# Attention banks, GpSimd's share and a direct first expert chunk in a three-stage kernel on one Trainium2 core

## Chip, core and metric

The kernel runs on one core of a Trainium2 chip. The metric is device time in microseconds (us) of one execution. Below, PE is TensorE, ACT is ScalarE, DVE is VectorE, POOL is GpSimd and SP is SyncE, which issues all DMAs.

## What is computed

Three layers follow each other on 2 x 768 = 1536 tokens of width 512:

```python
# 1. attention in chunks of 32 queries, with 16 keys to the left, 8 to the right and 8 memory keys
scores = scale * q_c @ k_full.T
a = exp(scores - max(scores)); a = a / (sum(a) + 1e-09)
out[:, :, chunk] = a @ v_full
# 2. a feed-forward layer, d_ff = 2048, with a rational activation
h = x @ w_in
P = a[0] + a[1]*h + a[2]*h**2 + a[3]*h**3
Q = 1 + abs(b[0])*abs(h) + abs(b[1])*h**2
x = (P / (Q + 1e-6)) @ w_out
# 3. four experts, d_ff = 1024, all applied to all tokens, weighted by normalised domain_probs
out = sum(p[:, e:e+1] * (relu(x @ w1[e]) @ w2[e]) for e in range(4))
```

Everything is float32 in and out; `w_in` and `w_out` arrive as 64-bit floats and are turned into 32-bit ones by three integer operations on DVE (L349, L355, L361).

## The kernel before

**Precision.** Each operand of a large product is split into a high half, rounded by a copy on ACT (L278), and a low half, the difference, on POOL or DVE (L323). A product of two tiles is three matmuls: high x high, low x high, high x low (`PAIRS`). All large matmuls are 128x128 by 128x512.

**Attention.** The work is cut into 24 units of 64 rows by 2 heads and 4 chunks (`Unit`), eight per block of 512 tokens. A unit loads its keys, queries and values into one tile `w`, then goes through scores on PE (L421, L424), the maximum on DVE (`peaks`, L430), its scaling (`peaks2`, L436), four exponentials on ACT (L440), addition of 1e-9 and reciprocal (`norm1`, L446, and `norm2`, L449), the normalisation on POOL (`norm3`, L453), the transposition on PE (L459), the copy of the probabilities on ACT or DVE (`probs`, L278, L279) and the product with the values on PE (L476). ACT and DVE then write the high and low halves of x (L545, L550). Each unit takes three PSUM banks. `psum_buf` gives units of block 0 (0 to 7) six banks in turn, two of tag `att` and four of tag `acc`; later units have the two `att` banks.

**Stage A** (layer 2) has 48 steps `StepA`: a block and a tile f of 128 hidden columns. The first product (`first_ops`, L566) has 12 matmuls into a bank `h` or `att`; the activation runs through ACT, DVE and POOL (L630 to L664), among it `ln`, the linear term B1*|h| + B0 (L656, ACT) and the product `de` on POOL (L660); its halves g feed the second product (`second_ops`, L672) of 12 matmuls into four `acc` banks, `LAG` = 3 steps later. Four tiles f go round the three blocks, then the next four in the opposite order, so that the blocks end in the order `LAST` = PA, PB, LONE (blocks 2, 1, 0): PA is complete eight steps, PB four steps before the end.

**Stage B** (layer 3) has 16 chunks `Chunk` of two tiles f of one expert. For PA and PB together the first product of a chunk is a 2 x 2 block product done with seven products (`product`, L786, 6 matmuls each) of sums of x (`plan_sums_x`, L717) and sums of weights (`plan_sums_w`, L717), put together on DVE (`plus`, L842). LONE has two direct products (L566, 12 matmuls each). ACT and DVE form the halves of relu (`gated`, L881, L884). Then each block has a second product of 24 matmuls over four `acc` banks (`second`, L905), which DVE adds to the output (L920 in chunk 0, L922 later).

**What sets the order.** All operations are given to a planner (`Plan`) with the engines on which each may run and a cost for each. PE's operations have keys, which `tick` hands out in a list written by hand. The planner then lists the operations: of those that can start, the earliest, and among equals the most urgent. Every engine runs its list in that order, and DMAs are issued by SP in that order too. Rings of buffers (`BUFS`) are taken in the order of need. At the start, before and between attention work, zero products of 128x512 (`turn_over`, L291) keep PE occupied where the plan has a gap, up to the unit `FU`:

```python
for a, b in zip(pe, pe[1:]):
    if a.n == last:
        break
    n = int((b.start - a.end - FGAP) / 0.216)
    if n > 0:
        fill[a] = min(n, 16)
```

Here `last` is the one zero product that is planned behind the values of unit `FU`.

## Time and profile before

| what | us |
|---|---|
| median of three runs | 863.58 (862.87 to 864.3) |
| the profiled execution | 864.07 |
| its span, first to last instruction | 862.2 |
| outside the span | 1.87 |
| PE busy | 837.8 (97%) |
| DVE busy | 637.8 (74%) |
| ACT busy | 380.3 (44%) |
| POOL busy | 339.9 (39%) |

The profile is of one execution. Matmuls overlap, so that a busy PE is not PE at its peak: twelve matmuls in a row are read best from the distance between the starts of such rows. A "releaser" is the instruction whose end the waiting one needed last. Times are counted from the start of the span. Attention lies in the first 104 us, stage A goes to about 325 us with its last second products behind that, stage B to the end.

### The profile page before, as it was taken

The numbers are of one execution on the slowest core, as the hardware profiler recorded it, in microseconds if no ns is written. First come the engines' busy times: TensorE is split into PE (matmuls) and PEld (weight loads), VectorE is DVE, ScalarE is ACT, GpSimd is POOL, SyncE is SP. The second block draws the span as 40 slices with busy tenths as digits, with TensorE's granted clock in tenths as the row PEclk, the third lists the DMA queues.
The fourth block names the chain that finished last, engine by engine and source line by source line (L and its number), as shares of the span: only waits on it lengthen the run. The fifth ranks groups of instructions, "written<-read, shape, count | busy, mean of one in ns | idle before, by whom it ended". The sixth has DMA issues, their size and how long they took to land.

```text
span 862.2 us, 11387 instructions
## 1 busy us (share of the span) xinstructions
PE 837.8 (97%) x4205; PEld 666.9 (77%) x4208; DVE 637.8 (74%) x982; ACT 380.3 (44%) x819; POOL 339.9 (39%) x273
## 2 busy tenths in 40 slices
PE   7899999999999997899999999999999999999998
PEld 5676788888888885688888888888888888888886
DVE  6988798999988779974766766765765765765754
ACT  6988887867778766420320320320330330330310
POOL 3454476656667759800330330330330330330300
PEclk9889999999999999999999999999999999999999
DMA  9966021212122001110101101101101101100003
GB/s 345 370 208 233 2 98 50 73 50 74 49 74 65 10 0 51 49 49 1 49 1 49 49 1 49 50 2 48 49 5 46 49 12 38 49 20 6 2 1 146
DMA packets 21912, 55.42 MB, mean 64 GB/s; under 512 B 3936, under 2 KB 3936, under 8 KB 21856
## 3 DMA queue, kind: packets, MB, share of 16 engines
q1 hardware_dynamic: 21856, 54.69, 18.6%
q8 instruction: 33, 0.54, 0.3%
q14 instruction: 23, 0.19, 0.1%
HBM read 51.54 MB, written 3.15 MB: 63 GB/s over the span
## 4 chain that ended last, share of the span: by engine, by line
PE 85%; DVE 5%; ACT 4%; DMA 2%; POOL 2%; issue 1%; SPq 0%; ACTq 0%; POOLq 0%; DVEq 0%
PE acc L905 30%; PE att L566 16%; PE acc L672 13%; PE h L786 9%; PE h L566 8%; PE att L786 7%; ACT w L440 1%; ACT w L278 1%; DMA w<-q 1%; DMA w<-qk 1%; DVE w L323 1%; POOL tu L717 1%; POOL w L323 0%; DVE ts L647 0%; DMA stg<-w 0%
## 5 line engine op out<-in xcount | busy, mean ns | idle before, releaser
L323 POOL TENSOR_TENSOR w<-stg,w 128x512 fp32r<-128x512 f32 x64 | 96.5, 1518 | 331.5 <-ACT w L278 331.5
L922 DVE SCALAR_TENSOR_TENSOR p<-acc,pr,p 128x512 f32<-128x512 f32 x180 | 135.1, 751 | 107.1 <-PE acc L905 106.8
L905 PE MATMUL acc<-w,g 128*128 128x512 f32 x768 | 181.8, 397 | 1.6 <-DVE p L920 1.6
L905 PEld LDWEIGHTS acc<-w,g 128*128 128x128 f32 x768 | 144.8, 189 | 36.1 <-issue 2.0
L566 PE MATMUL att<-x,w 128*128 128x512 f32 x612 | 149.3, 395 | 0.5 <-DVE ts L842 0.5
L672 PE MATMUL acc<-g,w 128*128 128x512 f32 x576 | 145.4, 398 | 1.9 <-POOL g L323 1.8
L566 PEld LDWEIGHTS att<-x,w 128*128 128x128 f32 x612 | 114.6, 187 | 29.1 <-issue 0.9
L672 PEld LDWEIGHTS acc<-g,w 128*128 128x128 f32 x576 | 107.3, 188 | 28.5 <-POOL g L323 2.7
L278 ACT ACTIVATE ts<-h 128x512 f32<-128x512 f32 x16 | 9.6, 598 | 246.1 <-PE h L786 246.1
L905 PE MATMUL acc<-w,gb 128*128 128x512 f32 x384 | 92.0, 397 | 0.0
L566 PE MATMUL h<-x,w 128*128 128x512 f32 x348 | 90.8, 406 | 0.0
L905 PEld LDWEIGHTS acc<-w,gb 128*128 128x128 f32 x384 | 72.5, 189 | 17.0
L323 POOL TENSOR_TENSOR g<-ts,g 128x512 fp32r<-128x512 f32 x48 | 68.5, 1428 | 38.5 <-ACT g L278 38.1
L660 POOL TENSOR_TENSOR ts<-ts,tu 128x512 f32<-128x512 f32 x48 | 63.6, 1325 | 43.6 <-ACT ts L656 40.1
L566 PEld LDWEIGHTS h<-x,w 128*128 128x128 f32 x348 | 65.2, 192 | 15.3
L786 PE MATMUL h<-x,w 128*128 128x512 f32 x192 | 50.3, 396 | 2.3 <-ACT g L278 1.6
L786 PE MATMUL att<-x,w 128*128 128x512 f32 x192 | 50.1, 395 | 1.0 <-DVE ts L647 1.0
L786 PE MATMUL h<-w 128*128 128x512 f32 x192 | 49.2, 391 | 0.7 <-DVE w L323 0.7
L323 POOL TENSOR_TENSOR w<-y,w 128x512 fp32r<-128x512 f32 x34 | 47.3, 1395 | 4.4 <-ACT w L278 3.6
L786 PEld LDWEIGHTS h<-x,w 128*128 128x128 f32 x192 | 35.8, 187 | 11.7 <-ACT g L278 2.0
L278 ACT ACTIVATE w<-tu 128x512 fp32r<-128x512 f32 x32 | 20.1, 632 | 53.8 <-POOL tu L717 49.6
L786 PEld LDWEIGHTS att<-x,w 128*128 128x128 f32 x192 | 35.9, 188 | 9.8 <-DVE ts L647 1.4
(114 smaller groups left out, 1188.2 us busy)
## 6 DMA issues: line engine op xcount, KB each, us to landing
stg<-w SPq DMA_DIRECT2D x64, 512.0 KB, 3.6
w<-kv SPq DMA_DIRECT2D x32, 256.0 KB, 5.6
w<-q SPq DMA_DIRECT2D x16, 256.0 KB, 5.3
w<-qk SPq DMA_DIRECT2D x8, 400.0 KB, 6.2
out<-p SPq DMA_DIRECT2D x12, 256.0 KB, 2.0
w<-v SPq DMA_DIRECT2D x8, 256.0 KB, 7.3
pr<-prob SPq DMA_DIRECT2D x1, 24.0 KB, 3.8
cf<-coef SPq DMA_DIRECT2D x1, 3.0 KB, 7.0
```

Of the source, the lines that this page charges most:

```text
L278: return lambda o, i: ACT.activation(o, i, AF.Copy)
L323: engines[op.eng].tensor_tensor(out=dst[:, 1], in0=src, in1=dst[:, 0].bitcast(F32), op=ALU.subtract)
L440: ACT.activation(k(n), P1.ap[:, n * KB : (n + 1) * KB], AF.Exp, scale=SCALE, bias=nm()[:, n : n + 1], accum_out=sm()[:, n : n + 1],)
L566: PE.matmul(s.h.ap, wt[w].ap[:, 0, a, k * 128 : (k + 1) * 128], xs[k].ap[:, b], start=(k == 0 and n == 0), stop=(k == KT - 1 and n == 2),)
L660: lambda: POOL.tensor_tensor(out=s.ap, in0=s.ap, in1=u.ap, op=ALU.mult), [ln], [s, u],
L672: PE.matmul(ps, wt[f].ap[:, 1, a, d * 128 : (d + 1) * 128], g.ap[:, b], start=start, stop=stop)
L717: lambda: engines[o.eng].tensor_tensor(out=out(), in0=in0(), in1=in1(), op=op),
L786: PE.matmul(ps.ap, left(a, k), right(b, k), start=k == 0 and n == 0, stop=k == 1 and n == 2,)
L905: PE.matmul(ps.ap, gs[j][0].ap[:, a, d * 128 : d * 128 + 128], wt[f].ap[:, 1, b], start=j == 0 and n == 0, stop=j == 1 and n == 2,)
L922: DVE.scalar_tensor_tensor(out=y, in0=ps.ap, scalar=p, in1=y, op0=ALU.mult, op1=ALU.add)
```

## The change

It consists of these parts:

- **Banks.** `psum_buf` gives the six banks in turn to units 0 to 11 (`RU` = 12), not 0 to 7.
- **Small operations.** `peaks2` and `norm1`, 128x4 each and 24 of each, go from DVE to POOL.
- **Linear term.** `ln` may run on ACT or POOL; the planner chooses. It puts 31 of 48 on POOL.
- **Zero products** are placed up to unit 11, in place of 5: 20 in all, in place of 16.
- **Direct first chunk.** Chunk 0 of stage B forms the first products of PA and PB directly (`direct`), four of 12 matmuls for seven of 6, and needs no sums. They stand between the last three second products of stage A. The splits of x now cover all 12 tiles (10 before) and are planned ahead of the sums of x.
- **Costs.** A matmul counts 0.2325 in the plan (`MM`), and the costs of many operations are other numbers; two lines of that are shown.

```diff
+MM = 0.2325
-FU = 5
+FU = 11
+RU = 12
...
             self.hp, self.half = divmod(r, 2)
 
         def psum_buf(self):
-            if self.blk:
+            if self.u >= RU:
                 return bank("att")
             Unit.turn = (getattr(Unit, "turn", -1) + 1) % 6
             return bank((["att"] * 2 + ["acc"] * 4)[Unit.turn])
...
                 )
             def peaks2():
-                DVE.tensor_scalar(out=nm(), in0=nm(), scalar1=SCALE, scalar2=None, op0=ALU.mult)
+                POOL.tensor_scalar(out=nm(), in0=nm(), scalar1=SCALE, scalar2=None, op0=ALU.mult)
             def exps():
                 for n in range(NQ):
...
                     )
             def norm1():
-                DVE.tensor_scalar(out=sm(), in0=sm(), scalar1=1e-9, scalar2=None, op0=ALU.add)
+                POOL.tensor_scalar(out=sm(), in0=sm(), scalar1=1e-9, scalar2=None, op0=ALU.add)
             def norm2():
                 DVE.reciprocal(out=sm(), in_=sm())
...
-            o1 = add([("PE", 0.68)], scores, [*ready, o_mask, o_ident], [T], [P1], key=t_scores)
+            o1 = add([("PE", 0.75)], scores, [*ready, o_mask, o_ident], [T], [P1], key=t_scores)
             o = add([("DVE", 0.33)], peaks, [o1], [P1], [st])
-            o = add([("DVE", 0.07)], peaks2, [o], [st])
+            o = add([("POOL", 0.15)], peaks2, [o], [st])
...
     def first_ops(s, w, xs, ready, t):
-        s.h = bank("h" if s.i < 2 * GS[0] + 3 or s.i % 4 < 2 else "att")
+        s.h = bank(s.tag if hasattr(s, "tag") else "h" if s.i < 2 * GS[0] + 3 or s.i % 4 < 2 else "att")
         def go(k):
             for n, (a, b) in enumerate(PAIRS):
...
                     after, uses,
                 )
+            def linear():
+                if ln.eng == "ACT":
+                    ACT.activation(s.ap, u.ap, AF.Identity, scale=B1, bias=B0)
+                else:
+                    POOL.tensor_scalar(out=s.ap, in0=u.ap, scalar1=B1, scalar2=B0, op0=ALU.mult, op1=ALU.add)
+
             ln = add(
-                [("ACT", 0.7)],
-                lambda: ACT.activation(s.ap, u.ap, AF.Identity, scale=B1, bias=B0), [ab], [u], [s],
+                [("ACT", 0.7), ("POOL", 0.75)],
+                linear, [ab], [u], [s],
             )
             de = add(
                 [("POOL", 1.23)],
...
                 )
 
             self.g = {}
+            if not c:
+                self.direct(("h", "att", "h", "att"), (PA, PB))
+                self.direct(("h", "att"), (LONE,))
+                return self.seconds()
             m1, p1 = product(1, "h")
             self.gate = p1
             u2 = Buf("ts", [128, BLK], F32)
...
             m4, p4 = product(4, "h")
             c21, o21 = plus(u3, m4, [o22, p4])
             self.gated(1, PA, c21, [o21], "g")
-            for j, f in enumerate(self.fs):
-                r = SimpleNamespace(i=1002)
-                o = first_ops(
-                    r, f, [x2[LONE, k] for k in range(KT)], [x_ready[LONE, k, 3] for k in range(KT)],
-                    t["F", j],
-                )
-                self.gated(j, LONE, r.h, [o], "gb")
-            for b in sorted(LAST, key=lambda b: t["S", b]):
+            self.direct(("att", "att"), (LONE,))
+            self.seconds()
+
+        def direct(self, tags, blocks):
+            tags = list(tags)
+            for b in blocks:
+                for j, f in enumerate(self.fs):
+                    r = SimpleNamespace(tag=tags.pop(0))
+                    o = first_ops(
+                        r, f, [x2[b, k] for k in range(KT)], [x_ready[b, k, 3] for k in range(KT)],
+                        self.t["F", b, j],
+                    )
+                    if b != LONE:
+                        self.gate = getattr(self, "gate", o)
+                    self.gated(j, b, r.h, [o], "gb" if b == LONE else "g")
+
+        def seconds(self):
+            for b in sorted(LAST, key=lambda b: self.t["S", b]):
                 self.second(b)
 
         def gated(self, j, blk, h, after, tag):
...
             chunks[c].order(tick, x)
     def a_second():
-        t2[ending.pop(0)] = tick(2.592)
+        t2[ending.pop(0)] = tick(12 * MM)
     seven = [("P", i) for i in (1, 2, 6, 7, 5, 3, 4)]
-    products(0, *seven[:2])
-    a_second()
-    products(0, *seven[2:5])
-    a_second()
-    products(0, *seven[5:])
-    a_second()
-    products(0, ("S", PA), ("S", PB), ("F", 0), ("F", 1))
+    lone = ("F", LONE, 0), ("F", LONE, 1)
+    for b in (PA, PB):
+        for j in range(2):
+            products(0, ("F", b, j))
+            if ending:
+                a_second()
+    products(0, ("S", PA), ("S", PB), *lone)
     products(1, *seven)
     products(0, ("S", LONE))
-    products(1, ("F", 0), ("F", 1), ("S", PA), ("S", PB), ("S", LONE))
+    products(1, *lone, ("S", PA), ("S", PB), ("S", LONE))
     for c in range(2, NC):
-        products(c, *seven, ("F", 0), ("F", 1), ("S", PA), ("S", PB), ("S", LONE))
+        products(c, *seven, *lone, ("S", PA), ("S", PB), ("S", LONE))
     prs = Buf("tm", [128, NT // 128], F32)
     o_ident = add([("POOL", 1.0)], lambda: make_identity(nc, ident))
...
     for i in range(nA):
         steps[i].plan(t1[i], t2[i])
-    plan_sums_x()
     for b in LAST:
         for k in range(KT):
-            if b == PB and k < 2:
-                continue
             x2[b, k] = Buf("x", [128, 2, BLK], F32R)
             x_ready[b, k, 3] = split(
                 lambda b=b, k=k: part[b].ap[:, k], lambda b=b, k=k: x2[b, k].ap,
                 [x_ready[b, k, 2]], [part[b]], takes=[x2[b, k]], fast=True,
             )
+    plan_sums_x()
     o = add([("SP", 0.1)], load_probs, [steps[nA - 1].firsts[0]])
     o_probs = add([("DVE", 0.7)], set_probs, [o], [], [prs])
     for c in range(NC):
         for j in range(2):
             plan_w32(2 * c + j)
-        plan_sums_w(c)
+        if c:
+            plan_sums_w(c)
     for c in chunks:
         c.plan()
     for o in list(plan.ops):
...
     for a, b in zip(pe, pe[1:]):
         if a.n == last:
             break
-        n = int((b.start - a.end - FGAP) / 0.216)
+        n = int((b.start - a.end - FGAP) / MM)
         if n > 0:
             fill[a] = min(n, 16)
     with tc.manual_schedule():
```

The change of costs and keys moves instructions. At the passage from stage A to stage B, PE's list before reads as follows (L672 second product of stage A, L786 one of the seven products, L566 direct product, L905 second product of stage B):

```order
L672 MATMUL acc<-g,w 128x512 x12
L786 MATMUL h<-x,w 128x512 x6
L786 MATMUL att<-x,w 128x512 x6
L672 MATMUL acc<-g,w 128x512 x20
L786 MATMUL h<-w 128x512 x12
L672 MATMUL acc<-g,w 128x512 x4
L786 MATMUL h<-x,w 128x512 x6
L672 MATMUL acc<-g,w 128x512 x6
L786 MATMUL att<-w 128x512 x3
L786 MATMUL att<-x,w 128x512 x6
L786 MATMUL att<-w 128x512 x3
```

and now (L680, L794, L568 and L927 are the same lines):

```order
L680 MATMUL acc<-g,w 128x512 x12
L568 MATMUL h<-x,w 128x512 x12
L680 MATMUL acc<-g,w 128x512 x12
L568 MATMUL att<-x,w 128x512 x12
L680 MATMUL acc<-g,w 128x512 x12
L568 MATMUL h<-x,w 128x512 x12
L680 MATMUL acc<-g,w 128x512 x12
L568 MATMUL att<-x,w 128x512 x12
L927 MATMUL acc<-w,g 128x512 x48
L568 MATMUL h<-x,w 128x512 x12
L568 MATMUL att<-x,w 128x512 x12
```

The second products of stage A (x12) now alternate with the four direct products of PA and PB, and the seven products of chunk 1 begin only behind 48 second products of chunk 0 and the two direct products of LONE. In the whole program PE has 3366 large matmuls, in place of 3360.

In the start, POOL's list around units 8 and 9 before (w_150 and w_154 are their tiles, st their statistics, L453 `norm3`, L660 `de`, L323 a low half):

```order
L453 TENSOR_TENSOR w_150<-w_150,st_421 128x256
L453 TENSOR_TENSOR w_154<-w_154,st_462 128x256
L323 TENSOR_TENSOR w_542<-y_437,w_542 128x512
L453 TENSOR_TENSOR w_359<-w_359,st_549 128x256
L660 TENSOR_TENSOR ts_601<-ts_601,tu_577 128x512
L660 TENSOR_TENSOR ts_640<-ts_640,tu_618 128x512
L453 TENSOR_TENSOR w_373<-w_373,st_635 128x256
L453 TENSOR_TENSOR w_470<-w_470,st_661 128x256
L323 TENSOR_TENSOR w_717<-y_575,w_717 128x512
```

and now (w_150 and w_175 are units 8 and 9; L438 `peaks2`, L448 `norm1`, L455 `norm3`, L659 the linear term, L668 `de`, L325 a low half):

```order
L438 TENSOR_SCALAR st_448<-st_448 128x4
L438 TENSOR_SCALAR st_484<-st_484 128x4
L448 TENSOR_SCALAR st_448<-st_448 128x4
L325 TENSOR_TENSOR w_495<-y_423,w_495 128x512
L659 TENSOR_SCALAR ts_531<-tu_517,cf_63 128x512
L455 TENSOR_TENSOR w_150<-w_150,st_448 128x256
L448 TENSOR_SCALAR st_484<-st_484 128x4
L668 TENSOR_TENSOR ts_531<-ts_531,tu_517 128x512
L455 TENSOR_TENSOR w_175<-w_175,st_484 128x256
L438 TENSOR_SCALAR st_570<-st_570 128x4
L325 TENSOR_TENSOR w_533<-y_493,w_533 128x512
L659 TENSOR_SCALAR ts_622<-tu_585,cf_63 128x512
```

Each unit now passes POOL three times, and the linear term stands ahead of `de` there. Up to the last unit's values PE's list holds 184 large matmuls, 168 before. ACT's list up to the last unit holds one linear term in place of 8, 36 copies of probabilities in place of 39, 12 high halves of weights in place of 10 and 8 of g in place of 7; DVE's list holds 13, 12 and 12 conversions in place of 10 each.

## Rows read from the trace of the kernel before

**Rows 1.** Windows by stage: busy us and instruction count by engine, granted clock, DMA.
```profile
core 0: us, PE busy (x) PEld busy (x) DVE busy (x) ACT busy (x) POOL busy (x), PEclk, DMA share, GB/s
...
24.58:104.16 79.58, 71.98 (x729) 53.57 (x725) 65.57 (x147) 71.68 (x238) 42.35 (x40) 0.94 0.60 206
104.16:325.39 221.23, 221.23 (x949) 178.26 (x949) 196.65 (x286) 165.62 (x278) 148.23 (x110) 1.00 0.16 53
325.39:372.63 47.24, 39.29 (x157) 28.27 (x156) 44.86 (x55) 21.52 (x38) 38.35 (x29) 1.00 0.20 68
372.63:858.50 485.87, 485.83 (x2089) 392.72 (x2087) 312.91 (x433) 104.80 (x185) 103.41 (x78) 1.00 0.09 31
...
37.83:48.48 10.65, 8.78 (x64) 6.34 (x63) 8.98 (x20) 9.18 (x36) 6.29 (x6) 0.52 0.83 293
```

**Rows 2.** Waits of PE, 24.58 to 104.16 us: total, times, longest.
```profile
PE att L476 <- ACT w L278: 3.2, 3, 1.6
PE att L421 <- DVE x L550: 1.7, 1, 1.7
PE att L459 <- POOL ts L660: 1.5, 1, 1.5
```

**Rows 3.** PE in order of time, start: start, length, what, count.
```profile
29.79 2.34 PE L566 MATMUL h<-x,w 128*128 128x512 f32 x9
...
34.56 0.69 PE L424 MATMUL att<-w 128*64 128x64 f32 x16
...
37.95 1.12 PE L424 MATMUL att<-w 128*64 128x64 f32 x16
...
44.54 4.01 PE L566 MATMUL h<-x,w 128*128 128x512 f32 x9
```

**Rows 4.** Chain that ended last, dense stretch: start, length, what.
```profile
311.56 2.80 PE acc L672 x12
```

**Rows 5.** Waits of PE, 325.39 to 372.63 us.
```profile
PE acc L905 <- DVE p L920: 1.6, 1, 1.6
```

**Rows 6.** ScalarE's groups, 24.58 to 104.16 us: busy and mean ns, idle before.
```profile
L278 ACT ACTIVATE w<-att 64x256 f32<-64x256 f32 x32 | 12.1, 378 | 0.5 <-PE att L459 0.2
...
L656 ACT ACTIVATE ts<-tu,cf 128x512 f32<-128x512 f32 x8 | 6.6, 821 | 0.1
...
L278 ACT ACTIVATE w<-y 128x512 fp32r<-128x512 f32 x9 | 5.5, 633 | 0.9 <-DVE y L361 0.7
```

**Rows 7.** VectorE's groups, 24.58 to 104.16 us.
```profile
L436 DVE TENSOR_SCALAR st<-st 128x4 f32<-128x4 f32 x15 | 7.4, 491 | 0.3
...
L446 DVE TENSOR_SCALAR st<-st 128x4 f32<-128x4 f32 x17 | 3.9, 228 | 3.5 <-ACT w L440 3.5
```

**Rows 8.** VectorE's groups, 104.16 to 325.39 us: the three conversions.
```profile
L355 DVE SCALAR_TENSOR_TENSOR y<-stg,y 128x512 int32<-128x512 int32 x22 | 20.8, 945 | 0.0
L361 DVE SCALAR_TENSOR_TENSOR y<-stg,y 128x512 int32<-128x512 int32 x22 | 19.6, 890 | 0.1
L349 DVE TENSOR_SCALAR y<-stg 128x512 int32<-128x512 int32 x22 | 17.0, 781 | 2.4 <-POOL w L323 2.4
```

**Rows 9.** Groups of the whole span, shapes apart.
```profile
L660 POOL TENSOR_TENSOR ts<-ts,tu 128x512 f32<-128x512 f32 x48 | 63.6, 1325 | 43.6 <-ACT ts L656 40.1 <-DVE tm L635 2.3 <-DVE st L436 0.6
...
L453 POOL TENSOR_TENSOR w<-w,st 128x256 f32<-128x256 f32 x24 | 16.9, 705 | 33.1 <-PE att L459 10.5 <-DVE st L449 7.0 <-DMA w<-kv 5.0
...
L291 PE MATMUL acc<-tm 128*128 128x512 bf16 x13 | 4.6, 514 | 1.2 <-DVE tm L287 1.2
...
L483 POOL TENSOR_SCALAR w<-w 128x64 f32<-128x64 f32 x4 | 1.3, 327 | 6.8 <-DMA w<-qk 6.8
```

**Rows 10.** All engines in order of time, dense stretch.
```profile
204.87 1.60 POOL L323 TENSOR_TENSOR g<-ts,g 128x512 fp32r<-128x512 f32 x1
...
205.24 1.52 DVE L349 TENSOR_SCALAR y<-stg 128x512 int32<-128x512 int32 x1
...
216.44 0.41 DVE L349 TENSOR_SCALAR y<-stg 128x512 int32<-128x512 int32 x1
```

More of the change, by code (lines that the diff above doesn't have):

```diff
@@ L328, in split @@
         lo = add(
-            [("POOL", 1.23), ("DVE", 0.6)] if fast else [("POOL", 1.23)],
+            [("POOL", 1.23), ("DVE", 1.0)] if fast else [("POOL", 1.23)],
             lambda: split_low(lo, dst(), src()), [hi], list(uses) + list(takes), lock=True,
@@ L364, in conv3 @@
                 )
-            ld = add([("SP", 0.77)], load, [], [], [r])
+            ld = add([("SP", 1.34)], load, [], [], [r])
             o = add([("DVE", 0.34)], conv1, [ld], [r], [y], lock=True)
@@ L379, in plan_w32 @@
         ld = add(
-            [("SP", 1.46)], lambda: SP.dma_start(out=r.ap.rearrange("p a b -> p (a b)"), in_=w32[n]),
+            [("SP", 1.34)], lambda: SP.dma_start(out=r.ap.rearrange("p a b -> p (a b)"), in_=w32[n]),
             [], [], [r, wt[f]],
@@ L508, in plan @@
             if blk == 0:
-                ld = add([("SP", 1.14)], load, [], [], [T])
+                ld = add([("SP", 1.05)], load, [], [], [T])
                 ready = [ld]
-                ready.append(add([("DVE", 0.3), ("ACT", 0.47), ("POOL", 0.53)], spread_k, [ld], [T], lock=True))
+                ready.append(add([("DVE", 0.36), ("ACT", 0.47), ("POOL", 0.53)], spread_k, [ld], [T], lock=True))
                 ready.append(add([("DVE", 0.1), ("ACT", 0.15), ("POOL", 0.25)], spread_m, [ld], [T], lock=True))
             else:
-                ld = add([("SP", 1.46)], load_qk, [], [], [T])
+                ld = add([("SP", 1.34)], load_qk, [], [], [T])
                 ready = [ld]
-            lv = add([("SP", 0.73)], load_v, [ld], [T])
-            o1 = add([("PE", 0.68)], scores, [*ready, o_mask, o_ident], [T], [P1], key=t_scores)
+            lv = add([("SP", 0.67)], load_v, [ld], [T])
+            o1 = add([("PE", 0.75)], scores, [*ready, o_mask, o_ident], [T], [P1], key=t_scores)
             o = add([("DVE", 0.33)], peaks, [o1], [P1], [st])
-            o = add([("DVE", 0.07)], peaks2, [o], [st])
+            o = add([("POOL", 0.15)], peaks2, [o], [st])
             o = add([("ACT", 1.16)], exps, [o], [P1, st, T])
-            o = add([("DVE", 0.07)], norm1, [o], [st])
+            o = add([("POOL", 0.15)], norm1, [o], [st])
             o = add([("DVE", 0.09)], norm2, [o], [st])
@@ L529, in plan @@
                 add(
-                    [("ACT", 0.27), ("DVE", 0.33)] if blk == 0 else [("ACT", 0.27)],
+                    [("ACT", 0.39), ("DVE", 0.45)] if blk == 0 else [("ACT", 0.39)],
                     lambda j=j: probs(j), [o2], [P2, T],
@@ L608, in second_ops @@
             o = add(
-                [("PE", 0.216 * len(grp))], lambda grp=grp: go(grp), need, [wt[w], s.g] + old, new, key=t
+                [("PE", MM * len(grp))], lambda grp=grp: go(grp), need, [wt[w], s.g] + old, new, key=t
             )
-            t += 0.216 * len(grp)
+            t += MM * len(grp)
             s.seconds.append(o)
@@ L708, in exact @@
         lo = add(
-            [("POOL", 1.23 * cost), ("DVE", 0.7 * cost)],
+            [("POOL", 1.23 * cost), ("DVE", 1.0 * cost)],
             lambda: split_low(lo, dst(), src()), [hi], list(uses) + list(takes), lock=True,
@@ L715, in combine @@
         o = add(
-            [("POOL", 1.23 * cost), ("DVE", 0.7 * cost)],
+            [("POOL", 1.23 * cost), ("DVE", 1.0 * cost)],
             lambda: engines[o.eng].tensor_tensor(out=out(), in0=in0(), in1=in1(), op=op),
@@ L791, in product @@
                 o = add(
-                    [("PE", 0.693)], go, [o, *need[k]], uses[k] + [ps] * k, [ps] * (1 - k),
-                    key=self.t["P", i] + 0.693 * k,
+                    [("PE", 3 * MM)], go, [o, *need[k]], uses[k] + [ps] * k, [ps] * (1 - k),
+                    key=self.t["P", i] + 3 * MM * k,
                 )
```

18 lines of the change are left out of this document (9 added, 9 removed).

## The prediction

> **What bounds the kernel now.** I read the windows by stage first, then what TensorE (PE) waited for, then its rows in order of time, then the groups of the other engines. PE sets the time nearly everywhere: from 104.16 to 325.39 us and from 372.63 to 858.50 us it has next to no idle time [rows 1], and there 12 products take 2.80 us, 0.2333 us each [rows 4]. Only work or waits in the two other stretches can be won.
>
> The first is the start, 24.58 to 104.16 us, where the attention of blocks 1 and 2 stands between the first expert products. PE waits 7.4 us there, 6.4 of it in the three rows shown [rows 2], and in 37.83 to 48.48 the granted clock is 0.52, the lower of its two levels, 1.2 in place of 2.4 GHz [rows 1]; PE had waited 1.7 us just before, on a bank [rows 2]. At the lower level nine products take 4.01 us, not 2.34, and a unit's scores 1.12, not 0.69 [rows 3]. With the two sets of scores that is 1.67 + 2 x 0.43 = 2.5 us lost. Visible loss of the stretch: 7.4 + 2.5 = 9.9 us. ScalarE (ACT) is the fullest engine, 71.68 of 79.58 us; VectorE (DVE) has 65.57, GpSimd (POOL) 42.35 [rows 1].
>
> The second is the passage from stage A to stage B, 325.39 to 372.63 us. The order of before holds 36 + 48 + 48 + 24 = 156 products there, 36.4 us at the dense pace, in 47.24 us: 10.8 us lost. PE waits for the low halves of g, for the sums of chunk 0, and for DVE's finishing of an output bank, the wait that is shown [rows 5]. DVE is busy 44.86 and POOL 38.35 of the 47.24 us [rows 1].
>
> **The change part by part.**
>
> *Direct first chunk.* Chunk 0 loses seven products of 6 matmuls and gets four direct ones of 12 for blocks PA and PB: 48 for 42, six more, **+1.4 us** of PE. It also loses the weight sums of chunk 0, and the sums of x are first read by chunk 1, behind two output sums of 24 products and two lone products. In the order the last three second products of stage A now alternate with direct products of PA and PB, whose only new inputs are the splits of x. PA's part is complete eight steps before the end of A, PB's four. So the 10.8 us of waits lose their cause, with one exception: both orders fill all four output banks twice in a row, and the 1.6 us wait on DVE's finishing [rows 5] I leave standing. Sum: -10.8 + 1.4 + 1.6 = **-7.8 us**. Bounds: no wait at all, -9.4; or DVE, which has only 2.4 us idle there, remains the limit, when its idle time alone can go, -2.4 + 1.4 = -1.0. I take a value near the first: the work that DVE keeps is the same, but the sums of x may now end some 36 us after the last second product of step 44 (13 items of 2.8 us) rather than at once.
>
> *Linear term.* The order puts 31 of 48 on POOL, 7 of the first 8 among them. ACT saves 0.821 us for each in the start [rows 6]. On POOL the operation does not occur; its ends are 0.327 us for a TENSOR_SCALAR of 64 elements per partition and 1.325 for an operation that reads two times 512 [rows 9]. I take 0.70, the row of 0.705 for one that reads two times 256 and so as many elements as this [rows 9]. In the dense stretch POOL has 73 us free [rows 1], so 24 of these add at most 24 x 1.325 = 31.8 us there; I cost them at nothing.
>
> *Small operations.* 48 tiny operations leave DVE. In the start 15 of the first kind took 0.491 us each and 17 of the second 0.228 [rows 7], 11.2 us together. On POOL each costs between nothing and 0.327 us [rows 9]; a unit's chain gains two changes of engine. Because POOL has 37 us idle in the start and PE waits there for ACT rather than for POOL [rows 2], I put nothing on the path for this. If the cover is gone, 32 x 0.327 = 10.5 us is the most it could add.
>
> *Banks.* Units 8 to 11 rotate over six banks instead of two, so the 1.7 us wait for DVE's x rows [rows 2] goes. What is late next there is the copy of the probabilities on ACT (3.2 us).
>
> *Zero products.* 20 in place of 16; four more, at most 0.514 us each [rows 9], placed where PE is expected to wait for attention. I cost them at nothing, 2.1 us if those gaps are gone. They should keep the 2.5 us of slow clock away.
>
> *Sum for the start.* Up to the last unit ACT has 7 linear terms and 3 copies less, 2 weight halves and one g half more (0.63 each): -7 x 0.821 - 3 x 0.378 + 3 x 0.633 = -5.0 us [rows 6]. DVE has 11.2 us less and about 8.7 more: conversions of 2 further weight tiles (3 x 0.781 + 2 x 0.945 + 2 x 0.890 = 6.0 [rows 8]) and some copies and step operations (2.7); -2.5. The order also places 16 more products before the last unit's values (184 for 168). I take **-5.0 us**, the relief of the fullest engine. Bounds: all of the visible loss, -9.9; or nothing.
>
> *Other edits.* New costs and keys only move instructions; their effect is in the orders counted above. The end of the program is the same.
>
> 864.07 - 7.8 - 5.0 = 851.3 us against the profiled execution. That one lies 0.49 us above the median of the three runs, so I predict **850.8 us**.
>
> **A rule against the change.** A DVE conversion that began while a POOL operation ran took 1.52 us, one that began with POOL free 0.41 us [rows 10]. The Trainium skill (SBUF — State Buffer, section "SBUF: two separate sides") says that GpSimd and some DVE operations share a port pair, that the one which starts first holds it for its whole length and that the other is blocked; the trace agrees with 1.52 against 0.41. It also says that only a DVE operation with two SBUF inputs, or in a mode that uses both ports, is concerned; by that the conversions pay and the five step operations, which read a PSUM bank, do not. The conversions are 20.8 + 19.6 + 17.0 = 57.4 us of DVE in the dense stretch [rows 8], 26% of it, so a linear term of 0.70 us costs DVE 0.18 us on average, 24 of them 4.4 us, and DVE has 24.6 us idle [rows 1]. So the sum stays; where every operation is paid in full it does not, which is the slower rival.
>
> **Rivals.**
> 1. *DVE still limits the passage* (for it: 44.86 of 47.24 us busy; against: the deadlines moved by some 36 us). The passage gives 1.0 us instead of 7.8: 850.8 + 6.8 = 857.6 us. Chance 0.15.
> 2. *The start gives nothing*, because each unit's chain now passes POOL three times, in order behind operations of 1.3 us (for it: PE already waits once for POOL, 1.5 us [rows 2]). 850.8 + 5.0 = 855.8 us. Chance 0.12.
> 3. *The zero products don't hold the clock*, so that part of the change does not do what it says: 2.5 us stay, 853.3 us. Chance 0.08.
> 4. *Rivals 1 and 2 together*: 862.6 us, no change. Chance 0.05.
> 5. *Slower: the port.* Every POOL operation that is added takes its full length from DVE. Start: 7 x 1.325 + 48 x 0.327 = 25.0 us against 14.0 us of DVE idle and 2.5 of relief, 8.5 over. Dense stretch: 31.8 against 24.6, 7.2 over. With the passage at -7.8 that is +7.9, and the start's 5.0 does not come: 863.6 + 7.9 = 871.5 us. It decides once DVE loses over about 86% of each operation's length. For it: the 1.52 us conversion. Against: the step operations keep their means, and the price taken is the upper bound. Chance 0.05.
>
> **How the numbers follow.** The forecast has 0.55. It and rivals 1 to 3 lie below 861.9, so faster by over 0.2% (1.7 us, about what a measurement can tell from no change) has 0.55 + 0.15 + 0.12 + 0.08 = 0.90; within 0.2%, 0.05; slower, 0.05. The bounds of its two terms give at most 9.4 + 9.9 = 19.3 us; both at once are unlikely, so the range begins at 845.0, a gain of 18.6. It ends at 858.5, which takes in rivals 1 to 3 and leaves out rivals 4 and 5.
>
> **What would show it.** Right: PE's waits of the passage shrink from 10.8 us to about 1.6; the last second products of stage A follow each other with 2.8 us between; the lower clock near 40 us is gone; the linear terms on POOL take under 1 us; ACT's busy time in the start falls by some 5 us. Wrong: a wait for DVE or POOL between the direct products; a linear term near 1.3 us; waits of PE in the dense stretch, which had none; a second stretch at the lower clock; units whose exponentials wait long for POOL.

## The result and the profile after

The changed kernel takes 856.0 us (855.45 to 856.68, 4 runs) where the kernel before takes 863.58: a ratio of 0.9913, interval 0.9895 to 0.993. That is 7.6 us faster by the medians; the profiled execution, 855.45 us, is 8.6 faster than that of before. The forecast was 850.8, 12.8 us below the median of before. The direction and the range held; the size did not.

Three points divide the program well: the end of the second product of step 19 (before any loss in the dense stretch), that of step 44 (where stage A passes into stage B), and the end of the last product. An end is the start plus the length of its row in TensorE's rows in order of time; between steps 19 and 44 lie 25 steps of 5.6 us, 140.0 us without a loss.

| | step 19 | step 44 | last product | start | dense | passage |
|---|---|---|---|---|---|---|
| before | 185.55 | 325.55 | 858.47 | | | |
| changed | 180.23 | 323.77 | 849.88 | -5.3 | +3.5 | -6.8 |
| predicted | | | | -5.0 | 0 | -7.8 |

The last three columns are the differences to before: up to step 19, from there to step 44, and behind it. So the start gave what was forecast, the passage 1.0 us less, and the dense stretch, which I had costed at nothing, took 3.5 us back. Of the 5.3 us some 1.5 belong to the clock of this one execution (last section): x5, the same kernel once more, has 3.9.

The windows of the changed kernel, with columns as in [rows 1]: the start, the stretch of the lower clock, and the dense stretch:

```profile
24.58:104.16 79.58, 75.40 (x769) 56.36 (x766) 64.96 (x127) 69.01 (x235) 64.83 (x82) 1.00 0.63 217
37.83:48.48 10.65, 9.44 (x122) 7.14 (x124) 9.66 (x22) 10.53 (x40) 9.63 (x12) 1.00 0.85 300
104.16:323.77 219.61, 217.72 (x927) 173.62 (x927) 192.21 (x274) 149.78 (x252) 166.74 (x134) 1.00 0.16 53
```

The clock that was 0.52 in the second window [rows 1] is 1.00. In the start TensorE is fuller by the work it has drawn forward; ScalarE (ACT) has lost 2.7 us and GpSimd (POOL) has gained 22. What TensorE waited for, first in the start, then behind 104 us:

```profile
PE att L461 <- POOL w L455: 0.9, 1, 0.9
PE att L423 <- ACT w L442: 0.7, 1, 0.7
PE att L423 <- DVE x L552: 0.6, 1, 0.6
PE acc L478 <- DVE w L281: 0.4, 1, 0.4
...
PE acc L478 <- ACT w L280: 0.2, 1, 0.2
...
PE acc L680 <- DVE p L699: 1.6, 2, 0.9
PE att L568 <- DVE ts L649: 1.5, 1, 1.5
PE acc L927 <- DVE p L942: 0.5, 1, 0.5
```

The 3.2 us for the copies of the probabilities [rows 2] have become 0.4 and 0.2 (L281 on VectorE, L280 on ScalarE), the 1.7 us for the bank 0.6; 0.7 us now go to the exponentials (L442) and 0.9 to the normalisation on GpSimd (L455). Behind 104 us there are three waits, all for VectorE (DVE). The first is new and lies in the dense stretch: the head of a segment waits for a bank that an eviction must free. (A segment is four steps of one block, its head the first of them; the evictions are VectorE's four additions, L699, which take a segment's sums out of the banks.) TensorE's rows there, and VectorE's in the same time:

```profile
177.27 2.96 PE L680 MATMUL acc<-g,w 128*128 128x512 f32 x12
180.07 2.96 PE L568 MATMUL att<-x,w 128*128 128x512 f32 x12
182.87 1.22 PE L680 MATMUL acc<-g,w 128*128 128x512 f32 x3
184.78 2.36 PE L680 MATMUL acc<-g,w 128*128 128x512 f32 x9 [0.69 <-DVE p L699]
```

```profile
178.02 0.67 DVE L363 SCALAR_TENSOR_TENSOR y<-stg,y 128x512 int32<-128x512 int32 x1
178.62 1.79 DVE L357 SCALAR_TENSOR_TENSOR y<-stg,y 128x512 int32<-128x512 int32 x1
180.34 0.74 DVE L649 SCALAR_TENSOR_TENSOR ts<-ts,cf,h 128x512 f32<-128x512 f32 x1
181.00 0.75 DVE L649 SCALAR_TENSOR_TENSOR h<-tm,cf,h 128x512 f32<-128x512 f32 x1
181.66 1.88 DVE L699 TENSOR_TENSOR p<-acc,p 128x512 f32<-128x512 f32 x3
183.45 0.67 DVE L649 SCALAR_TENSOR_TENSOR ts<-ts,h 128x512 f32<-128x512 f32 x1
184.05 0.68 DVE L699 TENSOR_TENSOR p<-acc,p 128x512 f32<-128x512 f32 x1
```

Step 19 ends at 180.23, yet its first eviction begins at 181.66, behind two conversions (one of 1.79 us) and two step operations; the fourth begins at 184.05, after the head has come. The head of step 20 begins on three banks and waits; its end comes 6.9 us after that of step 19 instead of 5.6. At step 28 the same costs 2.1 us. VectorE's groups in the dense stretch (the last column is its idle time before them, by what ended it):

```profile
L357 DVE SCALAR_TENSOR_TENSOR y<-stg,y 128x512 int32<-128x512 int32 x20 | 22.2, 1111 | 0.1
L649 DVE SCALAR_TENSOR_TENSOR ts<-ts,cf,h 128x512 f32<-128x512 f32 x21 | 15.6, 742 | 14.4 <-ACT h L672 14.4
L699 DVE TENSOR_TENSOR p<-acc,p 128x512 f32<-128x512 f32 x20 | 12.6, 680 | 0.0
L649 DVE SCALAR_TENSOR_TENSOR ts<-ts,cf,att 128x512 f32<-128x512 f32 x17 | 12.6, 741 | 9.0 <-ACT att L672 9.0
```

VectorE no longer waits ahead of any eviction (L699): it is busy up to each of them. In the kernel before it still had 8.2 us there, in which it waited for TensorE:

```profile
L691 DVE TENSOR_TENSOR p<-acc,p 128x512 f32<-128x512 f32 x20 | 13.3, 686 | 8.2 <-PE acc L672 8.1
```

Of the changed kernel's 27.4 us of idle time, 23.4 lie ahead of the operation that needs ScalarE's reciprocal. The second conversion has risen from 945 [rows 8] to 1111 ns.

### The profile page after: what moved, and what is told of

It is laid out like the page before. It is cut to its first block, busy times and chain, and to the rows that moved or that the text cites. A ratio compares the mean times of both kernels' runs of the same rounds, so it can differ in the third digit from the quotient of the medians.

```text
span 853.7 us, 11342 instructions
## 1 busy us (share of the span) xinstructions
PE 835.5 (98%) x4214; PEld 665.2 (78%) x4218; DVE 624.7 (73%) x929; ACT 357.8 (42%) x783; POOL 380.6 (45%) x350
## 4 chain that ended last, share of the span: by engine, by line
PE 66%; DVE 21%; ACT 4%; DMA 3%; POOL 3%; issue 2%; SPq 0%; DVEq 0%; ACTq 0%; POOLq 0%
PE acc L927 31%; PE att L568 11%; PE h L794 10%; PE att L794 7%; DVE ts L649 4%; PE h L568 3%; PE acc L680 3%; DVE tm L637 2%; DVE tm L641 2%; DVE p L699 2%; DVE y L357 2%; DVE y L363 1%; DVE y L351 1%; DVE att L649 1%; DMA w<-kv 1%
## 5 line engine op out<-in xcount | busy, mean ns | idle before, releaser
L325 POOL TENSOR_TENSOR w<-stg,w 128x512 fp32r<-128x512 f32 x64 | 97.0, 1525 | 325.4 <-ACT w L280 325.4
L927 PE MATMUL acc<-w,g 128*128 128x512 f32 x768 | 182.0, 397 | 0.5 <-DVE p L942 0.5
L927 PEld LDWEIGHTS acc<-w,g 128*128 128x128 f32 x768 | 144.9, 189 | 35.1 <-DVE p L942 1.4
L568 PE MATMUL att<-x,w 128*128 128x512 f32 x624 | 151.9, 395 | 1.5 <-DVE ts L649 1.5
L680 PE MATMUL acc<-g,w 128*128 128x512 f32 x576 | 146.3, 399 | 2.1 <-DVE p L699 1.6
L568 PEld LDWEIGHTS att<-x,w 128*128 128x128 f32 x624 | 116.9, 187 | 30.5 <-DVE ts L649 1.9
L680 PEld LDWEIGHTS acc<-g,w 128*128 128x128 f32 x576 | 106.9, 188 | 29.9 <-DVE p L699 3.0
L280 ACT ACTIVATE ts<-h 128x512 f32<-128x512 f32 x15 | 9.0, 599 | 246.0 <-PE h L794 246.0
L568 PE MATMUL h<-x,w 128*128 128x512 f32 x384 | 98.2, 400 | 0.5 <-DVE ts L649 0.3
L927 PE MATMUL acc<-w,gb 128*128 128x512 f32 x384 | 92.0, 397 | 0.0
L927 PEld LDWEIGHTS acc<-w,gb 128*128 128x128 f32 x384 | 72.6, 189 | 16.9
L568 PEld LDWEIGHTS h<-x,w 128*128 128x128 f32 x384 | 70.8, 188 | 17.7 <-POOL w L325 0.6
L325 POOL TENSOR_TENSOR g<-ts,g 128x512 fp32r<-128x512 f32 x48 | 66.7, 1391 | 26.8 <-ACT g L280 26.3
L668 POOL TENSOR_TENSOR ts<-ts,tu 128x512 f32<-128x512 f32 x48 | 63.3, 1320 | 12.9 <-ACT ts L657 9.6
L325 POOL TENSOR_TENSOR w<-y,w 128x512 fp32r<-128x512 f32 x36 | 49.9, 1387 | 8.3 <-ACT w L280 8.0
L280 ACT ACTIVATE g<-ts 128x512 fp32r<-128x512 f32 x48 | 30.3, 631 | 39.9 <-DVE ts L649 39.8
L794 PE MATMUL h<-x,w 128*128 128x512 f32 x180 | 46.8, 395 | 0.0
L794 PE MATMUL att<-x,w 128*128 128x512 f32 x180 | 46.8, 395 | 0.0
L794 PE MATMUL h<-w 128*128 128x512 f32 x180 | 46.0, 391 | 0.0
L794 PEld LDWEIGHTS h<-x,w 128*128 128x128 f32 x180 | 33.8, 188 | 8.2
L794 PEld LDWEIGHTS att<-x,w 128*128 128x128 f32 x180 | 33.8, 188 | 8.0
```

The lines of the kernel that those rows point to most:

```text
L280: return lambda o, i: ACT.activation(o, i, AF.Copy)
L325: engines[op.eng].tensor_tensor(out=dst[:, 1], in0=src, in1=dst[:, 0].bitcast(F32), op=ALU.subtract)
L568: PE.matmul(s.h.ap, wt[w].ap[:, 0, a, k * 128 : (k + 1) * 128], xs[k].ap[:, b], start=(k == 0 and n == 0), stop=(k == KT - 1 and n == 2),)
L668: lambda: POOL.tensor_tensor(out=s.ap, in0=s.ap, in1=u.ap, op=ALU.mult), [ln], [s, u],
L680: PE.matmul(ps, wt[f].ap[:, 1, a, d * 128 : (d + 1) * 128], g.ap[:, b], start=start, stop=stop)
L794: PE.matmul(ps.ap, left(a, k), right(b, k), start=k == 0 and n == 0, stop=k == 1 and n == 2,)
```

## The experiments

The same three terms of every run whose steps keep their order; medians are against the runs of before on the same chip, which had 863.9 to 864.2 us. Each row is one profiled execution, and its first column carries that execution's clock: by the clock on record, in the first 25 us x4 ran at full clock, as the changed kernel's first profile did, x9 had 3.4 us at the lower level and the others 6.8.

| run | start | dense | passage | median us |
|---|---|---|---|---|
| x5 the change again | -3.9 | +3.6 | -6.8 | 856.5 |
| x3 direct alone | +0.1 | 0.0 | -8.9 | 854.9 |
| x4 start's parts alone | -4.8 | +3.4 | +0.3 | 863.7 |
| x8 direct, banks, zero products | -1.5 | 0.0 | -9.1 | 853.3 |
| x11 the change with old costs | -2.3 | 0.0 | -9.7 | 851.9 |
| x1 dense linear terms on ACT | -3.3 | +6.3 | -6.9 | 859.7 |
| x9 start's linear terms on ACT | -2.5 | +3.5 | -6.8 | 859.0 |
| x10 small operations on DVE | +1.3 | +3.4 | -7.0 | 862.0 |
| x6 a conversion left out | -4.0 | +0.9 | -7.9 | 853.0 |
| x2 other banks | -3.7 | +3.6 | -8.5 | 857.5 |

**The engine of the dense linear terms.** Order kept, only the engine changed:

```diff
     listed = plan.run()
+    for x in steps[8:]:
+        x.ln.eng = "ACT"
```

> The changed kernel with its order kept to the last instruction, but the linear terms of steps 8 to 47 (24 of them were on GpSimd, 0.854 us each) computed by ScalarE at the same place of the list. It asks where the 3.6 us went that the changed kernel gives back between 102.5 and 323.6 us. Theory A, the linear terms on GpSimd (they make its queue longer, VectorE waits 23.4 us in all for ScalarE's reciprocals behind it, and the conversions' means rose from 945 to 1111, 890 to 907 and 781 to 831 ns): the last second product of step 44 ends about 320 us in place of 323.6, VectorE's waits there fall toward the 8.5 us of before, 856.0 - 3.6 = 852.4 us. Theory B, VectorE has as much to do as before and TensorE comes 5.4 us earlier, so that it catches up with VectorE whatever GpSimd does: the waits at the ends of blocks stay, 855.5 to 856.5 us. Theory C, ScalarE becomes late with 24 x 0.7 = 17 us more: over 857 us.

Measured: 859.73 us, ratio 0.9946 (0.9933 to 0.9958); the stalls grew to 1.9 and 4.4 us. Some 1.5 us of the second are the clock: behind the wait the granted clock is 0.91 in 225 to 245 us, and seven matmuls follow each other by 0.43 us in place of 0.23. Theory C by the time. Theory A's signs did not come: VectorE still waits 23.9 us for the reciprocals, and the three conversions take 2890 ns together, 2849 in the change. So the linear terms on GpSimd are not what costs the dense stretch; in this order they save 3 us, the clock included.

**Other banks for the direct products.**

```diff
-                self.direct(("h", "att", "h", "att"), (PA, PB))
+                self.direct(("h", "h", "att", "att"), (PA, PB))
```

> The changed kernel with the banks of the four direct products of blocks PA and PB taken in the order h, h, att, att instead of h, att, h, att. Today the second product waits 1.51 us for the att bank of step 46, whose value VectorE finishes at 330.9 us, while the h bank of step 45 is free before. Theory A, the bank alone: the wait goes, 856.0 - 1.5 = 854.5 us. Theory B, VectorE is what is late there (34.72 of 40.44 us busy): the third or fourth product waits instead, or the bank of the outputs 0.5 us longer, 855.5 to 856.5 us.

Measured: 857.49 us, 0.9917 (0.9904 to 0.9931), no difference to the change. The wait of 1.5 us is gone, and the last products begin 1.5 us earlier than in x5, but the program ends only 0.3 us earlier. The last rows of TensorE, of x2 (span 854.9 us) and of x5 (span 855.2):

```profile
844.13 5.76 PE L927 MATMUL acc<-w,gb 128*128 128x512 f32 x24
```

```profile
845.67 5.76 PE L927 MATMUL acc<-w,gb 128*128 128x512 f32 x24
```

What follows the last product took 5.0 us here and 3.8 in x5: the last output transfer landed 3.2 us after its issue, in place of 2.0. In x2, x7 and x12, the runs with these banks, a packet of the DMA queue that the profile calls instruction runs during that transfer, in the other profiles none does; whether it is the cause was not tried.

**The parts by themselves.** x3 is the kernel before with the hunks of the direct chunk alone; x4 is the changed kernel without them:

```diff
+            if not c:
+                self.direct(("h", "att", "h", "att"), (PA, PB))
+                self.direct(("h", "att"), (LONE,))
+                return self.seconds()
...
-        plan_sums_w(c)
+        if c:
+            plan_sums_w(c)
```

> The kernel before with the direct first chunk alone: start, linear terms, small operations, banks of the units and costs as before. The prediction's term for this part was -7.8 us, of which the changed kernel shows 6.8 in the passage, with a wait of 1.51 us for a bank. Theory A, the parts are independent: 863.6 - 6.8 = 856.8 us, and the stretch up to the last second product of step 44 ends at 325.4 us as before. Theory B, the change needs GpSimd's and VectorE's relief from the other parts (VectorE was busy 44.86 of 47.24 us in the passage): gain of at most 3 us, 860.5 us or more.

> The changed kernel with chunk 0 as before (seven products, weight sums, sums of x first): what is left are the start's parts (banks, small operations and linear terms on GpSimd, zero products, costs). The prediction's term for the start was -5.0 us; the changed kernel has 5.4 at 102.5 us and 1.8 at 323.6 us. Theory A, the dense stretch gives back the same 3.6 us with chunk 0 as before: the gain is 1.8 us, 861.8 us. Theory B, what was given back comes from the direct chunk's earlier splits and conversions in the plan: 863.6 - 5.4 = 858.2 us. Theory C, the passage of before waits for VectorE and GpSimd and takes whatever comes early: no change, 863.5 us.

Measured: direct alone 854.94 us, 0.989 (0.9877 to 0.9904); the rest alone 863.69 us, 0.9992 (0.9983 to 1.0001). Alone, the direct chunk makes the passage 8.9 us shorter, more than both theories had, and TensorE's only wait left between 325 and 375 us is

```profile
PE acc L672 <- POOL g L323: 0.3, 1, 0.3
```

The start's parts alone gain 4.8 us, lose 3.4 in the dense stretch, and the rest, 1.0 by the profile, can hardly be told from no change in the times: theory C by the time, theory A by the dense stretch. All that the change brings is the direct chunk; what was added to it has not made it faster (0.991 in x5 against 0.989, the intervals overlap).

**The change again, as yardstick.** 

> The changed kernel once more, beside the others on the same chip, as their yardstick: 856 us. In the two runs that share its first 60 us, the eighth product of the experts ended 0.9 and 1.5 us later than in its own profile (59.38 and 60.02 for 58.51 us), at a mean granted clock of 0.993 and 0.995 for 0.999. Theory A, a slow stretch of the clock comes in some executions: the times spread by some 1.5 us and the median lies between 855.5 and 857.5. Theory B, that was the edit: 855.5 to 856.7 as before.

Measured: 856.5 us (855.61 to 857.04). Theory A: the spread is there, and it comes from the first 20 us (last section). From here on x5 is what the others stand against.

**Less work for VectorE.** The lowest three bits of the late weights are left out:

```diff
-            o.fn()
+            if o.start < units[-1].o3.start or o not in conv.values():
+                o.fn()
```

> The changed kernel, its order kept, without the third conversion of the weights behind the last unit (the lowest three bits of those weights are left out: 20 instructions of 907 ns, 18.1 us of VectorE). It asks whether VectorE's load costs the two stalls of 1.3 and 2.1 us that the changed kernel has at the heads of the steps 20 and 28 (a second product follows the one before by 6.9 and 7.7 us there in place of 5.6), where TensorE waits for the evictions. Theory A, VectorE is full: the lead of 5.3 us at step 19 is kept to step 44, 856.0 - 3.4 = 852.6 us. Theory B, it waits for the chain through GpSimd and ScalarE (23.4 us of waits for the reciprocals) and not for its own work: the stalls stay over 2.5 us together, 855 us or more.

Measured: 853.04 us, 0.9872 (0.9858 to 0.9887). Theory A, nearly: with 18 us of VectorE's work away, the first stall is gone and the second is 0.8 us; the passage is 1.1 us shorter than in x5. The four evictions now begin as step 19 ends at 181.56:

```profile
180.39 0.75 DVE L650 SCALAR_TENSOR_TENSOR ts<-ts,cf,h 128x512 f32<-128x512 f32 x1 [1.32 <-ACT h L673]
181.06 0.75 DVE L650 SCALAR_TENSOR_TENSOR h<-tm,cf,h 128x512 f32<-128x512 f32 x1
181.72 1.88 DVE L700 TENSOR_TENSOR p<-acc,p 128x512 f32<-128x512 f32 x3
```

Even here VectorE waits 1.32 us for the reciprocal ahead of the evictions: its load counts, and its fixed order with it.

**More room at the heads.** `swaps` gets 22 and 30, with the banks of x2:

> The changed kernel with the order h, h, att, att of the banks for the direct products, and with steps 22 and 30 added to the list of swaps: the last second product of a segment then goes ahead of a first product, so that two first products (5.6 us) instead of one (2.8) stand between it and the head of the next segment, whose banks the evictions must have freed. Theory A, the evictions are late by 1.3 and 2.1 us and no more: both stalls go, 856.0 - 3.4 - 1.4 = 851.2 us. Theory B, the second product that is moved ahead now waits for its own g, whose chain is as late as the evictions: the loss moves there, 854.5 us with the bank's gain alone, or more.

Measured: 854.03 us, 0.9884 (0.9869 to 0.9898). Both stalls went, but the head of step 32 then lost 1.4 us: half of theory A's gain.

**Direct chunk, banks and zero products, old costs.** `FU = 11` and the six banks up to unit 11 on x3:

> The direct first chunk on the kernel before, with the six banks up to unit 11 and the zero products up to unit 11, but linear terms, small operations and costs as before. Direct alone took 854.9 us where the kernel before took 864.2. Theory A, the two parts remove the slow clock (2.5 us) and the wait for a bank (1.7 us), and the evictions have their 8 us of slack in the dense stretch as before: 854.9 - 2.5 to 4.2 = 850.7 to 852.4 us. Theory B, a lead of TensorE at 102 us is given back in the dense stretch whatever the order is, as in the changed kernel: 854 to 855 us.

Measured: 853.26 us, 0.9877 (0.9863 to 0.9892). Between the theories: these two parts are worth 1.5 us at step 19, and nothing of it is lost later. The slow clock did not go entirely, as theory A had it: 3.4 us at the lower level are left near 52 us (granted clock 0.98 in 24.58 to 104.16), behind waits of 1.3 and 1.5 us for copies of the probabilities on ScalarE.

**The parts of the start.** Order kept; `x.ln.eng = "ACT"` for `steps[:8]`, and the 48 small operations put back on VectorE:

> The changed kernel, its order kept, with the linear terms of steps 0 to 7 computed by ScalarE (7 of the 8 were on GpSimd). The prediction took the start's gain from ScalarE's relief: 7 x 0.821 of the -5.0 us. It is read at step 19, before the first stall of the dense stretch: the second product of that step ends at 181.7 us in the run x5_changed_again (185.6 before). Theory A, ScalarE is what the start waits for: the lead of 3.9 us there falls by 4 to 6 us, to nothing or below. Theory B, the lead comes from banks, zero products and small operations (which alone, without the small operations, gave 1.5): the lead keeps 3 us or more. As the lead is given back in the dense stretch anyway, the total is 856 to 857 us by both as long as a lead of 0.5 is left, and later by what is missing below that.

> The changed kernel, its order kept, with the 48 small operations of the softmax back on VectorE. The prediction put nothing on the path for them on GpSimd, as PE waits in the start for ScalarE. Theory A, that holds: the end of step 19 stays within 0.5 us of 181.7, and the total at 856.5 us. Theory B, VectorE's 11 us (15 x 0.491 and 17 x 0.228) count, since it is then as full as ScalarE: step 19 ends 1 to 4 us later. Theory C, the small operations wait behind GpSimd's long ones on GpSimd and VectorE is better for them: step 19 ends earlier by over 0.5 us.

Measured: 859.01 us, 0.9937 (0.9925 to 0.995), and 861.96 us, 0.9975 (0.9966 to 0.9984). At step 19 the linear terms of the start are worth 1.4 us, between the theories (A had 4 to 6, B at most 0.9). As x9's profile had 3.4 us less of the lower clock than x5's, they are worth more than that; the medians, 859.0 and 856.5, say 2.5, where both theories had next to no difference in the total. The small operations are worth 5.1 (5.5 by the medians), more than theory B had; 3.4 us at the lower clock near 52 us, which x5 does not have, are part of it. The small operations on VectorE in x10:

```profile
L438 DVE TENSOR_SCALAR st<-st 128x4 f32<-128x4 f32 x16 | 5.3, 334 | 0.1
L448 DVE TENSOR_SCALAR st<-st 128x4 f32<-128x4 f32 x16 | 5.0, 311 | 0.1
```

and on GpSimd in x5:

```profile
L448 POOL TENSOR_SCALAR st<-st 128x4 f32<-128x4 f32 x16 | 5.5, 344 | 2.8 <-ACT w L442 1.6
L438 POOL TENSOR_SCALAR st<-st 128x4 f32<-128x4 f32 x16 | 5.0, 315 | 4.5 <-DVE st L432 4.4
```

In the mean they take the same time on either engine. The median of one is 0.16 us on VectorE and 0.23 on GpSimd, but on VectorE a few take up to 1.28 us. On VectorE they stand in a queue that is 70.27 us full of 79.58 in the start (65.19 in x5), with ScalarE at 67.35:

```profile
24.58:104.16 79.58, 72.85 (x752) 54.27 (x753) 70.27 (x156) 67.35 (x233) 51.42 (x48) 0.98 0.62 213
```

Both runs also settle a point of the dense stretch: with 1.4 and 5.1 us less lead at step 19, the same two stalls came, 3.5 and 3.4 us together, in x10 without any lead over the kernel before. It is not TensorE's lead that makes them.

**The old costs.** The change without its new numbers for the planner:

```diff
-MM = 0.2325
...
-                [("PE", 3 * MM)], lambda k=k: go(k), ...
+                [("PE", 0.648)], lambda k=k: go(k), ...
...
-            [("POOL", 1.23 * cost), ("DVE", 1.0 * cost)],
+            [("POOL", 1.23 * cost), ("DVE", 0.7 * cost)],
```

> The changed kernel with the costs of the kernel before in the plan (0.216 us for a matmul and so on): all other parts, the direct first chunk among them, as in the change. It asks whether the two stalls of the dense stretch come from the new costs, which fill the plan's gaps differently, or from the lead that meets a full VectorE. Theory A, the lead: the stalls at the heads of two segments stay with 2.5 us or more together, about 856 us. Theory B, the new costs: no stall, the second product of step 44 ends about 321 us, 852 to 853 us.

Measured: 851.86 us (851.52 to 852.56), 0.9857 (0.9844 to 0.9871): theory B, and the fastest of all, ahead of both kernels. Only the costs are other than in the change; by them the planner also puts 28 linear terms on GpSimd in place of 31, and the profile shows 23 zero products (16 in x5). Its rows at the two heads (the head of step 20 begins at 185.90, that of step 28 at 230.70):

```profile
180.30 2.96 PE L679 MATMUL acc<-g,w 128*128 128x512 f32 x12
183.10 2.96 PE L566 MATMUL att<-x,w 128*128 128x512 f32 x12
185.90 2.96 PE L679 MATMUL acc<-g,w 128*128 128x512 f32 x12
...
227.90 2.96 PE L566 MATMUL att<-x,w 128*128 128x512 f32 x12
230.70 2.96 PE L679 MATMUL acc<-g,w 128*128 128x512 f32 x12
```

VectorE's rows at the first of them, its waits in the dense stretch, and the window of that stretch:

```profile
181.21 1.28 DVE L355 SCALAR_TENSOR_TENSOR y<-stg,y 128x512 int32<-128x512 int32 x2
182.42 1.87 DVE L698 TENSOR_TENSOR p<-acc,p 128x512 f32<-128x512 f32 x3
184.21 0.73 DVE L647 SCALAR_TENSOR_TENSOR ts<-ts,cf,h 128x512 f32<-128x512 f32 x1
184.87 0.68 DVE L698 TENSOR_TENSOR p<-acc,p 128x512 f32<-128x512 f32 x1
```

```profile
L647 DVE SCALAR_TENSOR_TENSOR ts<-ts,cf,h 128x512 f32<-128x512 f32 x21 | 15.5, 739 | 7.4 <-ACT h L671 7.2
L698 DVE TENSOR_TENSOR p<-acc,p 128x512 f32<-128x512 f32 x20 | 12.9, 680 | 3.0 <-PE acc L679 2.9
L647 DVE SCALAR_TENSOR_TENSOR ts<-ts,cf,att 128x512 f32<-128x512 f32 x17 | 12.6, 741 | 6.0 <-ACT att L671 5.9
```

```profile
104.16:323.26 219.10, 219.10 (x953) 176.61 (x952) 196.61 (x278) 153.86 (x259) 162.95 (x132) 1.00 0.16 56
```

The first eviction starts at 182.42, before step 19 ends at 183.26, and VectorE even waits for TensorE ahead of some. It idles 13.1 us for reciprocals instead of 23.4, with nearly the same instructions in another order. It is even fuller than in the change, 196.61 of 219.10 us against 192.21 of 219.61, and its three conversions are slower together, 2932 ns against 2849, and yet TensorE waits for nothing behind 104 us. In the table every run with the new costs loses time in the dense stretch, and every run with the old ones (x3, x8, x11) loses none.

**A third swap.** `swaps` gets 34 as well:

> A version that is to beat both: the changed kernel with the order h, h, att, att of the direct products' banks and steps 22, 30 and 34 in the list of swaps. With 22 and 30 the stalls of 1.3 and 2.1 us at the heads of steps 20 and 28 went and one of 1.4 us came up at the head of step 32. Theory A, the third swap removes that one as well: 854.0 - 1.4 = 852.6 us. Theory B, VectorE has no time left and is late at the next head (step 36 or 40) by as much: 854 us.

Measured: 854.62 us, 0.9886 (0.9871 to 0.9901). Theory B: the stall of 1.4 us at step 32 went, 0.6 and 0.7 came at the heads of steps 40 and 44, and the waits went on into stage B. The waits behind 325 us:

```profile
PE acc L927 <- DVE p L942: 0.6, 1, 0.6
PE acc L927 <- DVE p L699: 0.4, 1, 0.4
```

## Why the prediction was right, and where it failed

**The passage: right in mechanism, 1.0 us off, for a reason I had not named.** The direct chunk took the waits' cause away. Alone it gave 8.9 us, and 9.7 with the change's other parts at the old costs, a little over the better end of my bounds (9.4): even the wait on the finishing that I left standing is gone there. In the change it gave 6.8, because the new order makes VectorE late there: 1.5 us for a bank of step 46 and 0.5 for the finishing. That wait between the direct products was one of my signs of being wrong, and so were the waits in the dense stretch. Rival 1, VectorE as the limit, was right to that extent and no further.

**The start: near in size by luck, wrong in reason.** The -5.0 us were worked out as "the relief of the fullest engine", ScalarE. Its busy time fell by 2.7 us only, and its linear terms are worth 1.4 to 2.5 us. The small operations, for which I had put "nothing on the path", are worth 5.1 in this order: the wait rows named ScalarE, but VectorE was nearly as full and each unit passes through it twice for them. These values do not add up, because each is measured with the others in place. Built up part by part they do: banks and zero products give 1.5 us (x8), the small operations and linear terms 0.8 more under the old costs (x11), the new costs, on which I had put nothing, another 1.6 (x5). So 5.1 us is the price of putting the small operations back into an order that was planned without them on VectorE, not what they gave. The lower clock near 40 us went as forecast, but not by the zero products alone: x8 and x10, which have them, show 3.4 us of it near 52 us.

**The failed step: "Other edits. New costs and keys only move instructions; their effect is in the orders counted above."** It was not counted. I looked at the orders of the start and the passage and took the dense stretch at nothing, by the sum of VectorE's idle time, 24.6 us. That sum was no reserve: 8.2 us of it lay ahead of the evictions, the new order leaves none there and 23.4 ahead of the reciprocals, and the evictions at the head of a segment have 2.8 us in which all four must be done. With the old costs the loss is zero, and the time, 851.86 us, lies 1.1 us above my forecast. That is partly luck, since two errors cancel: the start gave 2.3 us for 5.0, the passage 9.7 for 7.8. Against x11 the new costs spoiled 3.6 us in the dense stretch and 2.9 in the passage (6.8 instead of 9.7), against 1.6 that they gave in the start (3.9 in x5, 2.3 in x11).

**The port.** The slower rival did not come. The conversions did slow down, 945 to 1111 ns for the second, but not by the linear terms: without those on GpSimd it takes 1107 ns, and the kernel is slower (x1). My price of 0.70 us for a linear term was low: 0.854 in the dense stretch, and 1.05 in the start, where my sign of being right was under 1 us.

```profile
L659 POOL TENSOR_SCALAR ts<-tu,cf 128x512 f32<-128x512 f32 x24 | 20.5, 854 | 13.2 <-ACT tu L632 13.2
```

**What stays open.** Which of the new costs moves VectorE's order for the worse was not tried; nor was x11 with the other banks. That VectorE's work counts is shown by x6, that another order takes the stalls away, though VectorE is fuller, by x11; how much of the stalls of the change is load and how much is waiting for reciprocals in a fixed order, x6 does not separate.

## What to carry to other kernels

Where a planner writes the order, its numbers are part of the change: measure the parts with the old numbers and the new ones, since more exact durations (0.2325 us for a matmul that takes 0.2333, where 0.216 stood) can come with a worse order. An engine's idle time is a reserve only where it lies ahead of the instruction that others wait for; look at what stands in its queue before each eviction that frees a bank. And a wait row names the last releaser: in a fixed order a tiny operation on the other nearly full engine of the same chain can cost more than a big one on the engine that is named.

## What the runs showed of the hardware

The same first instructions do not run at the same clock in every execution. The window 5 to 15 us of the changed kernel, in its first profile and in x5:

```profile
5.00:15.00 10.00, 7.19 (x141) 5.42 (x140) 7.36 (x24) 7.76 (x46) 5.76 (x16) 1.00 1.01 390
```

```profile
5.00:15.00 10.00, 6.93 (x91) 5.43 (x90) 6.00 (x20) 6.61 (x38) 4.54 (x13) 0.66 0.99 383
```

At a granted clock of 1.00 step 19 ends at 180.23, at 0.66 at 181.69: 1.5 us, about the spread of its times. The kernel before does not tell whether that holds for it. Its window reads 1.00 with step 19 at 185.55, and x3, whose start is the same, reads 0.66 with 185.63, but the profile of before has no record of the clock ahead of 10.6 us, and the column counts that as full. Its rows there are those of the lower level: the scores of a unit take 1.12 us up to 9.8 us, not 0.69.

```profile
8.65 1.12 PE L424 MATMUL acc<-w 128*64 128x64 f32 x16 [0.27 <-POOL w L483]
```

The Trainium skill (TensorE: Matmul & The Clock Gate, "Part 1: The HAM clock gate") says that the number of slow matmuls at the start varies from run to run of one kernel. These runs agree: between 4 and 15 us the changed kernel has one such row of 1.12 us for a unit's scores in its first profile and three in x5. The kernel before has four, so that x5 is the nearer to compare it with.

A tensor-scalar operation of 128x4 takes 0.31 to 0.34 us in the mean on VectorE (x10) and on GpSimd (x5) alike, with medians of 0.16 and 0.23 us. The linear term on GpSimd takes 1.05 us in the start and 0.85 in the dense stretch, with the same shape.
